# A 4-tokens-per-partition beginning and crossbar-DMA transposes in a fused gated-linear-attention and squared-ReLU kernel

## Chip, cores, metric

The kernel runs on one core of one Trainium2 chip. The metric is the device time of one execution in microseconds (us). A profile of one execution gives the span from the first to the last instruction, about 2 us shorter than the device time. Runs are classed as fast or slow (slow: more than 1.5% above the fastest of the same kernel); ratios, intervals and the times quoted below are of fast runs alone.

## The reference, cut to what matters

```python
# 4 batches x 8 heads x 768 tokens x 48: gated linear attention, token by token
for t in range(S):
    state = alpha[:, :, t, :, None] * state + einsum('bhd,bhe->bhde', k[:, :, t], v[:, :, t])
    y[:, :, t] = einsum('bhd,bhde->bhe', q[:, :, t], state)
x = y.transpose(0, 2, 1, 3).reshape(3072, 384)
h = x @ w_in                  # 384 x 2048
out = relu(h) ** 2 @ w_out    # 2048 x 384, float32 in and out
```

## The kernel before

The recurrence is cut into 24 chunks of 128 tokens (six for each batch). For each chunk, prefix sums of log alpha turn decay into products; q and k are scaled by them, transposed (eight 128x128 blocks), and multiplied to scores; masked scores times v, plus q times the carried state, give x; x is transposed (three blocks) and goes through the two matmuls of the feed-forward part, called the expert matmuls below. A planner in Python simulates the engines with fixed durations and emits every engine's instructions in the order that it found. That order is static: TensorE takes its matmuls in it, and waits where one is not ready.

```python
srcs = [(n, a.rearrange("b h (c p) d -> b c p h d", p=P)) for n, a in srcs]   # 128 tokens x 8 runs of 192 B
...
    d["ld_" + nm] = add("DMA", LD, ld, prev, lat=2.0, at=0.6)        # all DMAs on the SP queue, in order
...
        def e_p1():                                  # eight transposes by TensorE into PSUM
            d["pT"] = ps_misc.tile([P, 2 * NP, P], BF16, name="misc")
            for p in range(NP):
                tr(d["pT"][:, p, :], qA[:, 2 * p:2 * p + 2, :], ident_bf)
            for p in range(NP):
                tr(d["pT"][:, NP + p, :], kI[:, 2 * p:2 * p + 2, :], ident_bf)
        p1 = plan.add(Op("PE", 0.47, e_p1, [mq, mk], takes=[sl_misc], **g))
        def e_cp():                                  # and a VectorE copy to SBUF
            d["qkT"] = work.tile([P, 2 * NP, P], BF16, name="qkT")
            pin(nc.vector.tensor_copy(d["qkT"], d["pT"]))
...
        p2 = plan.add(Op("PE", 0.42, e_p2, [cp], takes=[sl_sc], **g))    # scores
...
    GN = [2, 1, 1, 2, 2, 2, 2, 2, 2, 2, 2, 2, 2]     # chunks in each group of expert matmuls
    DMA_ORDER = [0, 1, "i", "i", "i", "i", 2, 3, "o", "o", "o", "o"]   # chunks, w_in, w_out
# (all else cut)
```

Of the kernel before, what the change touches and what calls it, by code (L numbers as in the profile page):

```python
# [19 lines left out]
class Slots:  # L20
# [5 lines left out]
    def free_at(self):  # L26
        n = len(self.release) - self.bufs
        if n < 0:
            return 0.0
        op = self.release[n]  # L30
        return None if op.done is None else op.done
# [10 lines left out]
class Plan:  # L42
# [30 lines left out]
    def run(self, gate):  # L73
        free = self.free
        while any(self.pending.values()):
# [23 lines left out]
            if eng == "OUT":  # L99
                free["DMA"] = max(free.get("DMA", 0.0), t) + op.dur  # L100
# [6 lines left out]
        self.order.sort(key=lambda o: o.start)  # L107
# [3 lines left out]
def kernel(  # L111
# [21 lines left out]
    NT = n_tok // P  # L133

# [40 lines left out]

    NBUF = 4
    L_s = big.tile([P, NBUF, H, DP], BF16)
    nc.gpsimd.memset(L_s[:, :, :, D:], 0.0)
    qA_s = big.tile([P, NBUF, H, DP], BF16)
    nc.gpsimd.memset(qA_s[:, :, :, D:], 0.0)  # L180
    kI_s = big.tile([P, NBUF, H, DP], BF16)
    nc.gpsimd.memset(kI_s[:, :, :, D:], 0.0)
    ae_s = big.tile([P, NBUF, NP, 2], FP32)
    nc.vector.memset(ae_s, 0.0)  # L184
    xT_big = big.tile([P, KT, n_tok], BF16)
# [11 lines left out]
    sl_misc, sl_sc, sl_h, sl_o = Slots(2), Slots(1), Slots(2), Slots(1)  # L197
    X_SLACK = 0.3
    LD = 1.08
    WLD = 2.2  # L200
    SQ_PRIO = 0.0
# [8 lines left out]
    def cast(dst, box, j, d, n):  # L210
        def e_cast():
            eng = nc.vector if op.eng == "DVE" else nc.gpsimd
            pin(eng.tensor_copy(dst, box["t"][:, j, :]))  # L213
        op = add({"DVE": 0.06 + n / 1840.0, "POOL": 0.05 + n / 660.0}, 0, e_cast, d, prio=1.0)
        return op

    def load_w_in(i):
        w = d_ff // NWP
        sl = slice(i * w, (i + 1) * w)
        box = {}  # L220

        def ld():
            box["t"] = wload.tile([P, KT * d_ff // NWP], FP32, name="wst").rearrange("p (j n) -> p j n", j=KT)
            nc.sync.dma_start(out=box["t"], in_=w_in_r[:, :, sl])

        d = add("DMA", WLD, ld, lat=2.0)
        cs = []
        for j in range(KT):
            cs.append(cast(w_in_b[:, j, sl], box, j, d, 512))
        w_in_ready.append(cs)  # L230

    def load_w_out(i):
# [9 lines left out]
        for j in range(w):  # L242
            cs.append(cast(w_out_b[:, i * w + j, :], box, j, d, d_model))
# [6 lines left out]
    def add_loads(s):  # L250
        d = C[s]
        b, c = divmod(s, NCH)
        for nm, src in srcs:
# [3 lines left out]
            prev = C[s - LB]["use_" + nm] if s >= LB else None  # L257
            d["ld_" + nm] = add("DMA", LD, ld, prev, lat=2.0, at=0.6)

    def add_chunk(s):  # L260
        d = C[s]
        b, c = divmod(s, NCH)
# [5 lines left out]

        def e_ln():
            pin(nc.scalar.activation(L[:, :, 0:D], d["at"], AF.Ln))  # L270
        ln = d["use_at"] = add("ACT", 0.41, e_ln, d["ld_at"], old, prio=-5.0)
        ln.chunk = s

        def e_vb():
            d["vb"] = work.tile([P, H, D], BF16, name="vb", bufs=4)
            pin(nc.gpsimd.tensor_copy(d["vb"], d["vt"]))  # L276
        vb = d["use_vt"] = add("POOL", 0.62, e_vb, d["ld_vt"], old, prio=-1.0)

        def e_p0():
            pm = d["pm"] = ps_misc.tile([P, 512], FP32, name="misc")  # L280
            mm(pm[:, 0:HD], lhsT=utri_b[:, 0, :], rhs=L[:, :, 0:D], start=True, stop=True)
            for p in range(NP):
                mm(pm[:, HD + p:HD + p + 1], lhsT=L[:, 2 * p:2 * p + 2, :], rhs=ones_col,
                   start=True, stop=True)
        p0 = Op("PE", 0.28, e_p0, [ln], takes=[sl_misc], **g)
        p0.gla = s

        def exp(out_t, lo, hi, sl, scale):
            pin(nc.scalar.activation(out_t, sl, AF.Exp, scale=scale))

        def e_A():
            d["A"] = work.tile([P, H, D], BF16, name="A")
            pin(nc.scalar.activation(d["A"], d["pm"][:, 0:HD].rearrange("p (h d) -> p h d", h=H), AF.Exp))  # L293

        def e_Ai():
            d["Ai"] = work.tile([P, H, D], BF16, name="Ainv")
            pin(nc.scalar.activation(d["Ai"], d["pm"][:, 0:HD].rearrange("p (h d) -> p h d", h=H), AF.Exp, scale=-1.0))  # L297

        def e_ae0():
            pin(nc.scalar.activation(ae[0:64, :, 0], d["pm"][0:64, HD:HD + NP], AF.Exp))  # L300

        def e_ae1():
            pin(nc.scalar.activation(ae[64:128, :, 1], d["pm"][64:128, HD:HD + NP], AF.Exp))
        plan.add(p0)
        a_ = add("ACT", 0.39, e_A, p0, **g)
        ai = add("ACT", 0.38, e_Ai, p0, a_, **g)
        ae0 = add("ACT", 0.18, e_ae0, p0, ai, **g)
        ae1 = add("ACT", 0.19, e_ae1, p0, ae0, **g)
        p0.gives = ae1

        def e_qA():
            pin(nc.vector.tensor_mul(qA[:, :, 0:D], d["qt"], d["A"]))  # L312

        def e_kI():
            pin(nc.vector.tensor_mul(kI[:, :, 0:D], d["kt"], d["Ai"]))  # L315
        mq = d["use_qt"] = add("DVE", 0.47, e_qA, a_, d["ld_qt"], old, **g)
        mk = d["use_kt"] = add("DVE", 0.47, e_kI, ai, d["ld_kt"], old, **g)

        def e_p1():
            d["pT"] = ps_misc.tile([P, 2 * NP, P], BF16, name="misc")  # L320
            for p in range(NP):
                tr(d["pT"][:, p, :], qA[:, 2 * p:2 * p + 2, :], ident_bf)
            for p in range(NP):
                tr(d["pT"][:, NP + p, :], kI[:, 2 * p:2 * p + 2, :], ident_bf)
        p1 = plan.add(Op("PE", 0.47, e_p1, [mq, mk], takes=[sl_misc], **g))

        def e_cp():
            d["qkT"] = work.tile([P, 2 * NP, P], BF16, name="qkT")
            pin(nc.vector.tensor_copy(d["qkT"], d["pT"]))  # L329
        cp = add("DVE", 0.61, e_cp, p1, **g)  # L330
        p1.gives = cp

        def e_p2():
            sc = d["sc"] = ps_sc.tile([P, 2, NP, P], FP32, name="sc")
            t = d["qkT"]
            for p in range(NP):
                for hh in range(2):
                    sl = slice(64 * hh, 64 * hh + 64)
                    mm(sc[:, hh, p, :], lhsT=t[sl, NP + p, :], rhs=t[sl, p, :], start=True, stop=True)
        p2 = plan.add(Op("PE", 0.42, e_p2, [cp], takes=[sl_sc], **g))  # L340

        def e_sm(hh):
            if hh == 0:
                d["sm"] = work.tile([P, 2, NP, P], BF16, name="sm")
            pin(nc.vector.tensor_mul(d["sm"][:, hh], d["sc"][:, hh], utri_b.to_broadcast([P, NP, P])))  # L345
        sm0 = add("DVE", 0.6, lambda: e_sm(0), p2, **g)
        sm1 = add("DVE", 0.6, lambda: e_sm(1), p2, sm0, **g)
        p2.gives = sm1

        ps = None  # L350
        if not last:
            def e_ps():
                if c == 0:
                    state["ps"] = ps_st.tile([P, NP, 2 * D], FP32, name="st")
                st = d["st"] = state["ps"]
                for p in range(NP):
                    mm(st[:, p, :], lhsT=kI[:, 2 * p:2 * p + 2, :], rhs=d["vb"][:, 2 * p:2 * p + 2, :],
                       start=(c == 0 and p == 0), stop=True, skip_group_check=True)
            prev = C[s - 1].get("sb") if s else None
            if c == 0 and s:  # L360
                prev = C[s - 2]["sb"]
            ps = plan.add(Op("PE", 0.17, e_ps, [mk, vb, ae1, prev], **g))
# [11 lines left out]
        def e_p3():  # L374
            py = d["py"] = ps_misc.tile([P, 512], FP32, name="misc")
            if c > 0:
                for p in range(NP):
                    mm(py[:, 2 * p * D:2 * (p + 1) * D], lhsT=d["qkT"][:, p, :], rhs=C[s - 1]["sbt"][:, p, :],
                       start=(p == 0), stop=False, skip_group_check=True)
            for hh in range(2):  # L380
                for p in range(NP):
                    h = 2 * p + hh
                    mm(py[:, h * D:(h + 1) * D], lhsT=d["sm"][:, hh, p, :], rhs=d["vb"][:, h, :],
                       start=(c == 0 and hh == 0 and p == 0), stop=True, skip_group_check=True)
        p3 = plan.add(Op("PE", 0.39, e_p3, [sm1, vb, C[s - 1]["sb"] if c else None], takes=[sl_misc], **g))
# [7 lines left out]
        def e_p4():  # L393
            d["px"] = ps_misc.tile([P, KT, P], BF16, name="misc")
            for j in range(KT):
                tr(d["px"][:, j, :], d["xn"][:, j * P:(j + 1) * P], ident_bf)
        p4 = plan.add(Op("PE", 0.18, e_p4, [xn], takes=[sl_misc], **g))
# [8 lines left out]
    GN = [2, 1, 1, 2, 2, 2, 2, 2, 2, 2, 2, 2, 2]  # L406
# [4 lines left out]
    NQ = 4  # L411
    M1_ALT = 3
# [7 lines left out]
    def add_moe1(g, f, before):  # L420
# [17 lines left out]
        rl = add("ACT", (72 + n) / 1200.0, e_relu, op, prio=RELU_PRIO if g > 1 else RELU_PRIO0)  # L438
        op.gives = rl
        def e_sq():  # L440
            if f == 0:
                gT[g] = big.tile([P, FT, 384], BF16, name=f"gT{g % 3}", tag=f"gT{g % 3}")
            eng = nc.vector if sq[(g, f)].eng == "DVE" else nc.gpsimd
            pin(eng.tensor_mul(gT[g][:, f, 0:n], box["r"][:, 0:n], box["r"][:, 0:n]))  # L444
        fr = sq[(g - 3, "free")] if g >= 3 else None
        first = sq[(g, 0)] if f else None
        sq[(g, f)] = add({"DVE": 0.05 + n / 1900.0, "POOL": 0.06 + n / 440.0}, 0, e_sq, rl, fr, first, prio=SQ_PRIO)
        return op

    def add_moe2(g, tt, before):  # L450
# [3 lines left out]
        for qd in range(NQ):  # L454
            def e_mm(qd=qd, me=None):
# [3 lines left out]
                for kf in range(qd * FT // NQ, (qd + 1) * FT // NQ):  # L459
                    mm(box["po"], lhsT=gT[g][:, kf, tt * P:(tt + 1) * P], rhs=w_out_b[:, kf, :],  # L460
                       start=(kf == 0), stop=(kf == FT - 1))
            deps = [sq[(g, f)] for f in range(FT)] + sum(w_out_ready, []) + [before if qd == 0 else op]
            op = plan.add(Op("PE", 2.56 / NQ, e_mm, deps, takes=([sl_o, sl_misc] if tail else [sl_o]) if qd == 0 else None, prio=0.1, lat=0.2))
# [3 lines left out]

            op.lat = 0.0 if qd < NQ - 1 else 0.2

        def e_ev():  # L470
            box["ob"] = opool.tile([P, d_model], FP32, name="ob")
# [91 lines left out]
```

## Time and profile before

| | before |
|---|---|
| time, median of 4 runs | 200.94 us |
| span of the profiled run | 198.8 us |
| first w_in matmul | 17.62 us |
| first w_out matmul | 42.10 us |
| TensorE idle from 60 to 180 us | 0.8 us |
| DMA engines full | to about 130 us |

The table of stretches of the kernel before gives, for each stretch in us, the busy time of TensorE, its weight loads, VectorE, ScalarE and GpSimd (instructions in brackets), then the granted TensorE clock, the busy share of the DMA engines, and the rate.

```profile
20.00:40.00 20.00, 17.69 (x210) 13.07 (x209) 17.89 (x47) 14.30 (x53) 11.92 (x23) 0.97 0.99 248
...
80.00:100.00 20.00, 20.00 (x220) 14.98 (x218) 14.42 (x26) 15.51 (x47) 12.56 (x21) 1.00 1.07 197
...
120.00:140.00 20.00, 20.00 (x226) 15.17 (x225) 12.77 (x25) 14.62 (x45) 12.01 (x20) 1.00 0.67 124
...
160.00:180.00 20.00, 20.00 (x214) 15.22 (x212) 10.44 (x21) 12.96 (x39) 11.29 (x19) 1.00 0.09 32
```

From 80 us on TensorE is busy 20.00 of 20 us: whatever TensorE does there is the time. The DMA engines are full too until about 130 us, and hardly used after it. The next lines, from the timeline of the kernel before (start, length, engine, line, operation), mark its beginning: the first expert matmul, and the first one with w_out.

```profile
17.62 1.33 PE L191 MATMUL ph<-xT_big,w_in_b 128*128 128x256 bf16 x6 [1.34 <-DVE xT_big L400]
...
42.10 2.76 PE L191 MATMUL po<-w_out_b,gT_340 128*128 128x384 bf16 x16
```

The page of the kernel before shows what the DMA engines carry, and the chain of work that ended last:

```profile
DMA packets 107035, 30.23 MB, mean 152 GB/s; under 512 B 100353, under 2 KB 105473, under 8 KB 107009
...
q1 hardware_dynamic: 107008, 29.89, 72.7%
...
PE 78%; ACT 5%; DVE 5%; DMA 4%; SPq 4%; issue 2%; POOL 2%; ACTq 0%; POOLq 0%; DVEq 0%
```

Nearly all packets are the 192 B runs of q, k, v and alpha. The chain is TensorE for 78%.

### The profile page before, as it was taken

The numbers are of one execution on the slowest core, as the hardware profiler recorded it, in microseconds if no ns is written. First come the engines' busy times: TensorE is split into PE (matmuls) and PEld (weight loads), VectorE is DVE, ScalarE is ACT, GpSimd is POOL, SyncE is SP. The second block draws the span as 40 slices with busy tenths as digits, with TensorE's granted clock in tenths as the row PEclk, the third lists the DMA queues.
The fourth block names the chain that finished last, engine by engine and source line by source line (L and its number), as shares of the span: only waits on it lengthen the run. The fifth ranks groups of instructions, "written<-read, shape, count | busy, mean of one in ns | idle before, by whom it ended". The sixth has DMA issues, their size and how long they took to land.

```text
span 198.8 us, 5351 instructions
## 1 busy us (share of the span) xinstructions
PE 186.3 (94%) x1973; PEld 136.1 (68%) x1976; DVE 130.3 (66%) x265; ACT 131.8 (66%) x396; POOL 101.5 (51%) x175
## 2 busy tenths in 40 slices
PE   7876987989999899999999999999999999999993
PEld 3444745757577688777777777877777777777661
DVE  0775888977789897776666677665857756713300
ACT  3523864866569899767877877776886776656510
POOL 5134654841146757755666566576475464465300
PEclk9997899999999999999999999999999999999999
DMA  6999999898999999899999999851101101100022
GB/s 123 186 350 347 166 250 378 199 206 173 198 195 213 195 173 192 170 214 195 197 179 210 196 197 207 167 114 40 41 3 40 42 1 46 40 38 19 27 79 79
DMA packets 107035, 30.23 MB, mean 152 GB/s; under 512 B 100353, under 2 KB 105473, under 8 KB 107009
## 3 DMA queue, kind: packets, MB, share of 16 engines
q1 hardware_dynamic: 107008, 29.89, 72.7%
q8 instruction: 15, 0.25, 0.6%
q14 instruction: 12, 0.09, 0.2%
HBM read 25.17 MB, written 4.72 MB: 150 GB/s over the span
## 4 chain that ended last, share of the span: by engine, by line
PE 78%; ACT 5%; DVE 5%; DMA 4%; SPq 4%; issue 2%; POOL 2%; ACTq 0%; POOLq 0%; DVEq 0%
PE po L191 29%; PE ph L191 28%; PE misc L191 10%; PE misc L194 6%; DMA wst<-in_moe_w_in_dram 4%; PE sc L191 4%; SPq L256 3%; ACT r L437 3%; PE st L191 1%; DVE gT_606 L444 1%; DVE w_out_b L213 1%; DVE gT_752 L444 1%; POOL gT_340 L444 1%; DVE qkT L329 1%; POOL gT_1148 L444 1%
## 5 line engine op out<-in xcount | busy, mean ns | idle before, releaser
L437 ACT ACTIVATE r<-ph 128x256 bf16<-128x256 f32 (+1 forms) x192 | 67.5, 374 | 30.7 <-PE ph L191 25.9
L191 PE MATMUL ph<-xT_big,w_in_b 128*128 128x256 bf16 (+1 forms) x576 | 81.6, 269 | 2.4 <-DVE xT_big L400 1.3
L191 PEld LDWEIGHTS <-w_in_b 128*128 128x128 bf16 x624 | 54.1, 99 | 17.3 <-issue 3.6
L345 DVE TENSOR_TENSOR sm<-sc,utri_b 128x512 bf16<-128x512 f32 x48 | 31.6, 685 | 5.2 <-PE sc L191 5.0
L276 POOL CAST vb<-vt 128x384 bf16<-128x384 f32 x24 | 13.3, 553 | 17.5 <-DMA vt<-in_v_dram 17.5
L312 DVE TENSOR_TENSOR qA_s<-qt,A 128x384 bf16<-128x384 f32 x24 | 13.9, 579 | 11.8 <-ACT A L293 11.4
L329 DVE COPY qkT<-misc 128x1024 bf16<-128x1024 bf16 x24 | 16.5, 689 | 5.6 <-PE misc L194 4.8
L293 ACT ACTIVATE A<-misc 128x384 bf16<-128x384 f32 x24 | 11.7, 488 | 9.0 <-PE misc L191 9.0
L315 DVE TENSOR_TENSOR kI_s<-kt,Ainv 128x384 bf16<-128x384 f32 x24 | 16.5, 687 | 1.1
L191 PEld LDWEIGHTS <-qkT 64*128 64x128 bf16 (+1 forms) x272 | 10.6, 95 | 7.0 <-DVE qkT L329 1.6
L270 ACT ACTIVATE L_s<-at 128x384 bf16<-128x384 f32 x24 | 12.5, 522 | 3.8 <-DMA at<-in_alpha_dram 3.7
L475 ACT COPY ob<-po 128x384 f32<-128x384 f32 x20 | 9.6, 478 | 6.6 <-PE po L191 6.2
L400 DVE COPY xT_big<-misc 128x384 bf16<-128x384 bf16 x24 | 8.5, 354 | 8.1 <-PE misc L194 8.0
L389 ACT CAST xn<-misc 128x384 bf16<-128x384 f32 x24 | 11.5, 479 | 3.2 <-PE misc L191 3.1
L191 PE MATMUL po<-warm 128*128 128x512 bf16 x37 | 10.9, 424 | 1.6 <-DVE ae_s L184 1.3
L371 ACT CAST sb<-st 128x384 bf16<-128x384 f32 x20 | 9.5, 477 | 3.9 <-DVE st L366 3.7
L297 ACT ACTIVATE Ainv<-misc 128x384 bf16<-128x384 f32 x24 | 12.0, 499 | 0.0
L366 DVE TENSOR_TENSOR st<-st,ae_s 128x384 f32<-128x384 f32 x20 | 11.1, 556 | 0.4 <-PE st L191 0.4
L444 POOL TENSOR_TENSOR gT_3206<-r 128x256 bf16<-128x256 bf16 x12 | 7.6, 639 | 6.2 <-ACT r L437 5.3
L444 POOL TENSOR_TENSOR gT_2317<-r 128x256 bf16<-128x256 bf16 x12 | 7.6, 639 | 5.7 <-ACT r L437 4.8
L444 POOL TENSOR_TENSOR gT_2008<-r 128x256 bf16<-128x256 bf16 x12 | 7.6, 639 | 5.6 <-ACT r L437 4.9
L444 POOL TENSOR_TENSOR gT_2923<-r 128x256 bf16<-128x256 bf16 x12 | 7.6, 642 | 5.5 <-ACT r L437 5.0
(92 smaller groups left out, 349.5 us busy)
## 6 DMA issues: line engine op xcount, KB each, us to landing
at<-in_alpha_dram SPq DMA_DIRECT2D x24, 192.0 KB, 4.3
qt<-in_q_dram SPq DMA_DIRECT2D x24, 192.0 KB, 4.3
kt<-in_k_dram SPq DMA_DIRECT2D x24, 192.0 KB, 4.6
vt<-in_v_dram SPq DMA_DIRECT2D x24, 192.0 KB, 4.2
out_dram<-ob SPq DMA_DIRECT2D x24, 192.0 KB, 2.1
wst<-in_moe_w_in_dram SPq DMA_DIRECT2D x4, 768.0 KB, 8.5
wst<-in_moe_w_out_dram SPq DMA_DIRECT2D x4, 768.0 KB, 8.9
```

What stands on the lines that cost most here:

```text
L191: pin(nc.tensor.matmul(*a, **kw))
L194: pin(nc.tensor.transpose(*a))
L270: pin(nc.scalar.activation(L[:, :, 0:D], d["at"], AF.Ln))
L276: pin(nc.gpsimd.tensor_copy(d["vb"], d["vt"]))
L293: pin(nc.scalar.activation(d["A"], d["pm"][:, 0:HD].rearrange("p (h d) -> p h d", h=H), AF.Exp))
L297: pin(nc.scalar.activation(d["Ai"], d["pm"][:, 0:HD].rearrange("p (h d) -> p h d", h=H), AF.Exp, scale=-1.0))
L312: pin(nc.vector.tensor_mul(qA[:, :, 0:D], d["qt"], d["A"]))
L315: pin(nc.vector.tensor_mul(kI[:, :, 0:D], d["kt"], d["Ai"]))
L329: pin(nc.vector.tensor_copy(d["qkT"], d["pT"]))
L345: pin(nc.vector.tensor_mul(d["sm"][:, hh], d["sc"][:, hh], utri_b.to_broadcast([P, NP, P])))
L437: pin(nc.scalar.activation(box["r"][:, 0:n], box["ph"][:, 0:n], AF.Relu))
L444: pin(eng.tensor_mul(gT[g][:, f, 0:n], box["r"][:, 0:n], box["r"][:, 0:n]))
```

## The change

Two ideas, both to take work or waiting from TensorE. First, the first chunks of all four batches need no state, so they are done together at the start, in a layout of four tokens to a partition: q, k and alpha then come in runs of 768 B, and four chunks of x are ready for the expert matmuls. Second, from the ninth chunk on, q, k and x are transposed by crossbar DMAs from SBUF to SBUF. The diff, cut to its core:

```diff
+    order = [b * NCH for b in range(B)] + [b * NCH + c for b in range(B) for c in range(1, NCH)]
+    QK_DMA = 8
+    X_DMA = 8
+    TR_LAT = 2.5                     # the planner's latency of a transpose after its 0.9 or 0.34 us
+    AHEAD = 3.0
-        self.order.sort(key=lambda o: o.start)
+        self.order.sort(key=lambda o: o.start - (ahead if o.eng == "DMA" else 0.0))
+    def add_first_loads(nm, ap, tag):
+            F[nm] = big.tile([P, H, J * D], FP32, name="first_" + nm, tag=tag)
+            src = ap[:, :, 0:P, :].rearrange("b h (i j) d -> b i h (j d)", j=J)
+            w = P // B
+            for b in range(B):
+                nc.sync.dma_start(out=F[nm][b * w:(b + 1) * w], in_=src[b])   # a band of 32 partitions
 ... (prefix sums over four tokens a partition, four chunks at once; k transposed back; masks: cut)
+            def e_tr():
+                d["qkT"] = work.tile([P, 2 * NP, P], BF16, name="qkT")
+                nc.sync.dma_start_transpose(out=d["qkT"], in_=qk_s[:, i].rearrange("p x h d -> p (x h d)"))
+            if s >= QK_DMA:
+                cp = add("TR", 0.9, e_tr, mq, mk, lat=TR_LAT, prio=-20.0)
+                return ae1, mk, [cp]
+        def e_trx():
+            nc.sync.dma_start_transpose(out=xT_big[:, :, s * P:(s + 1) * P], in_=d["xn"])
+        if s >= X_DMA:
+            d["x"] = d["end"] = add("TR", 0.34, e_trx, xn, lat=TR_LAT + X_SLACK, prio=-20.0)
+            return
-    GN = [2, 1, 1, 2, 2, 2, 2, 2, 2, 2, 2, 2, 2]
+    GN = [1, 1, 2, 2, 2, 2, 2, 2, 2, 2, 2, 2, 2]
-    DMA_ORDER = [0, 1, "i", "i", "i", "i", 2, 3, "o", "o", "o", "o"]
+    DMA_ORDER = ["v", "i", "i", "i", "i", 4, "o", "o", "o", "o"]
 ... (w_out matmuls of the first groups in two halves; casts on more engines: cut)
```

## The prediction

> **What bounds it now.** Two regimes. The table of stretches shows TensorE busy 20.0 of 20 us in every stretch from 80 to 180 us, and the chain of waits runs 78% on TensorE. So from about 45 us to the end the time is the sum of TensorE work. Before that TensorE waits: the timeline has its first expert matmul at 17.6 us (two chunks and four w_in pieces had to land first; dummies fill the gaps) and its first w_out matmul at 42.2 us. From matmul spacing in the timeline (one token tile: 16 w_out matmuls of 0.163 us and its share of w_in, 5.2 us; recurrence 1.8 us a chunk) useful work is about 24 x 7.0 = 168 us (estimate). The 198.8 us span therefore loses about 27 us, 3.4 of it at the tail and nearly all the rest before 42 us. DMA is full until about 130 us, at only 195 GB/s, because 100353 of 107035 packets are under 512 B; one 192 KB load then costs about 1.0 us, a chunk 4 us.
>
> **The change.**
> 1. *Beginning.* The first chunk of all four batches comes first; they need no state. q, k and alpha come in 768 B runs; at the 350 to 377 GB/s that the weight stretches show that is 2.2 us per tensor of four chunks, not 4. v stays at 1 us a load. Before the last w_in piece: 6.6 + 4 + 8.8 = 19.4 us of DMA, against 16.8 now. So the first expert matmul does not come earlier (18 to 20 us). But then four tiles, not two, are ready, and with half of w_out their second matmuls start (about 30 us, not 42). Added: block cumulative sums and k transposed back, about 3 us of TensorE. Estimated idle before saturation: 12 to 15 us instead of 24. Gain 9 to 12, less 3 of added work: 6 to 9 us.
> 2. *Transposes.* The timeline has eight q/k transposes taking 0.45 us of TensorE and three x transposes 0.17: 0.62 us a chunk, times 16 = 9.9 us, all in the saturated stretch. VectorE also loses 0.69 + 0.35 us of copies a chunk, which isn't critical.
> 3. *Cost.* 352 KB a chunk go through the DMA engines. The Trainium skill (DMA: Bandwidth & Descriptors, Latency and other measured facts) gives transposes 261 GB/s: an estimated 1.35 us a chunk, 22 us in all. DMA per chunk becomes 4.0 + 0.55 + 1.35 = 5.9 us, under TensorE's 6.4. No run here shows it yet. Latency is the danger: loads take 4.3 us from issue to landing on the same in-order queue, a transpose behind them probably 4 to 5, where the schedule allows 3.4. TensorE's order is fixed, so score matmuls may wait 0 to 1 us a chunk: I allow 4 us in all.
>
> **Prediction.** 168 + 3 - 10 = 161 us of work, 13 idle at the start, 3.4 tail, 4 of new waits: span about 181, time (2 us above the span) **183 us**, range **175 to 196**. Faster by over 2%: **0.90**; within 2%: **0.05**; slower: **0.05**.
>
> **Right if:** first w_out matmul near 30 us; TensorE full from about 36 us; matmul count down by about 176 for the transposes and up by some 70 at the start; each transpose DMA landing within about 5 us; DMA busy until 150 us or later; waits of TensorE for qkT or xT_big under 0.5 us each.
>
> **Wrong if:** transposes block other traffic or run far below 261 GB/s (two or three times the cost makes DMA, not TensorE, the limit and the gain vanishes); the SP queue, waiting for q/k products, holds loads back; or the 32-partition first loads run well below weight-load rate, which delays the start.

## The result, and the profile after

The time rose to 208.75 us (median of 4 runs, 208.0 to 209.67), against 200.94 us: ratio 1.039, 95% interval 1.034 to 1.044. Ratios are the mean time of one kernel's fast runs over that of the other's of the same rounds, so they are not quite the ratio of the medians quoted. The results are correct.

| | before | after |
|---|---|---|
| first w_in matmul | 17.62 us | 25.70 us |
| first w_out matmul | 42.10 us | 46.71 us |
| TensorE idle, 60 to 180 us | 0.8 us | 11.5 us |
| TensorE busy from 60 us to the end | 134.6 us | 133.1 us |
| DMA engines full | to 130 us | to about 160 us |

The same stretches of the changed kernel, and the page's lines on its DMA traffic and chain that answer to those shown before:

```profile
20.00:40.00 20.00, 17.83 (x225) 11.88 (x225) 16.72 (x41) 14.24 (x49) 10.47 (x19) 1.00 1.03 326
...
80.00:100.00 20.00, 17.65 (x168) 12.95 (x167) 12.32 (x30) 13.42 (x42) 5.72 (x9) 0.91 1.09 180
...
120.00:140.00 20.00, 17.82 (x190) 13.16 (x187) 13.03 (x31) 15.03 (x44) 4.99 (x8) 1.00 0.99 190
...
160.00:180.00 20.00, 17.98 (x179) 13.21 (x180) 12.73 (x28) 12.92 (x40) 3.91 (x6) 0.91 0.52 96
```

```profile
DMA packets 121369, 35.98 MB, mean 173 GB/s; under 512 B 111616, under 2 KB 119808, under 8 KB 121344
...
q1 hardware_dynamic: 121344, 35.66, 86.1%
...
PE 69%; DMA 20%; DVE 4%; ACT 3%; issue 1%; SPq 1%; ACTq 0%; DVEq 0%
```

TensorE, full before, now misses 2 us and more in each of these late stretches, and DMA has gone from 4% to 20% of the chain. The chain by line names the transposes: qkT 8.6% and xT_big 5.9% of the span. The timeline of the changed kernel shows its beginning,

```profile
25.70 0.34 PE L230 MATMUL po<-xT_big,w_in_b 128*128 128x128 bf16 x3
...
46.71 1.46 PE L230 MATMUL misc<-w_out_b,gT_398 128*128 128x384 bf16 x8
```

8 us and 4.6 us later than before, and one stall near the end of its loads (in time order, VectorE, SP and TensorE):

```profile
155.48 0.94 DVE L495 TENSOR_TENSOR qk_s<-kt,Ainv 128x384 bf16<-128x384 f32 x1
...
156.19 0.42 SPq L313 DMA_DIRECT2D qt<-in_q_dram  x1
...
156.72 2.06 SPq L507 DMA_TRANSPOSE qkT<-qk_s  x1
...
159.57 0.24 PE L230 MATMUL misc<-ones_col,L_s 128*128 128x1 bf16 x4
...
162.01 0.26 PE L230 MATMUL sc_3114<-qkT 64*128 64x128 bf16 x1 [2.21 <-DMA qkT<-qk_s]
...
162.53 1.46 PE L230 MATMUL po<-w_out_b,gT_2877 128*128 128x384 bf16 x4
```

The k product ends at 156.42 (155.48 + 0.94), SP issues the transpose at 156.72 but needs 2.06 us to get it into the queues, and the scores start 5.6 us after the product. The schedule had allowed 3.4 us (0.9 + 2.5). Over the sixteen chunks this distance is 3.2 to 5.9 us, median 4.6. The bracket says that TensorE sat idle 2.21 us. The last line shows a second price: four w_out matmuls take 1.46 us, where 0.81 is the normal length. The narrow stretches around it show the granted clock (column before the last two):

```profile
159.00:160.00 1.00, 0.81 (x9) 0.46 (x7) 0.58 (x2) 0.79 (x4) 0.00 (x0) 1.00 1.32 236
...
161.00:162.00 1.00, 0.00 (x0) 0.00 (x0) 0.00 (x0) 0.27 (x1) 0.00 (x0) 1.00 1.24 211
...
163.00:164.00 1.00, 1.00 (x6) 0.45 (x3) 1.00 (x3) 0.00 (x0) 0.00 (x0) 0.50 1.20 261
```

After the 2.21 us of idle the clock is at half for 3.4 us. It happened twice after 60 us (the other after a wait of 2.35 us that ended at 86 us); the clock of 0.91 in two of the 20 us stretches is that, 1.7 us of TensorE time each. The Trainium skill (TensorE: Matmul & The Clock Gate, Why this matters for your kernels) tells to leave no idle gaps over about 3 us; here 2.2 us was enough. The length of one gap doesn't decide it: among the runs below, half clock followed waits of 1.44 and 0.60 us close together in stride_tr (at 146.5 us), and did not follow a wait of 2.04 us in tr_lat5 (ended at 102.6 us).

From 60 us on the sums are: 9.9 us of transposes gone from TensorE, but about 4.9 us of work left over from the slower beginning (measured below without the transposes) and 3.4 us of half clock; so its busy time fell only 1.5 us, and its idle time rose by 10.7 us. That is the 9.2 us between the spans.

### The profile page after: what moved, and what is told of

Its sections match the earlier page's. It is cut to its first block, busy times and chain, and to the rows that moved or that the text cites. A ratio compares the mean times of both kernels' runs of the same rounds, so it can differ in the third digit from the quotient of the medians.

```text
span 208.0 us, 5075 instructions
## 1 busy us (share of the span) xinstructions
PE 184.7 (89%) x1816; PEld 131.0 (63%) x1817; DVE 130.8 (63%) x309; ACT 136.6 (66%) x399; POOL 61.1 (29%) x112
## 4 chain that ended last, share of the span: by engine, by line
PE 69%; DMA 20%; DVE 4%; ACT 3%; issue 1%; SPq 1%; ACTq 0%; DVEq 0%
PE ph L230 26%; PE po L230 23%; PE misc L230 11%; DMA qkT<-qk_s 9%; DMA xT_big<-xn 6%; DMA first_k_154<-in_k_dram 4%; PE misc L233 2%; DMA first_a_144<-in_alpha_dram 2%; ACT r L668 1%; PE st L230 1%; DVE qk_s L395 1%; DVE gT_398 L675 1%; DVE gT_642 L675 1%; SPq L326 1%; PE sc_289 L230 0%
## 5 line engine op out<-in xcount | busy, mean ns | idle before, releaser
L449 POOL CAST vb<-vt 128x384 bf16<-128x384 f32 x20 | 11.6, 578 | 13.8 <-DMA vt<-in_v_dram 10.8
L495 DVE TENSOR_TENSOR qk_s<-kt,Ainv 128x384 bf16<-128x384 f32 x20 | 14.3, 715 | 0.3
L613 ACT CAST xn<-misc 128x384 bf16<-128x384 f32 x24 | 11.5, 479 | 3.4 <-PE misc L230 3.4
L590 DVE TENSOR_TENSOR st<-st,ae_s 128x384 f32<-128x384 f32 x20 | 11.2, 561 | 1.4 <-PE st L230 1.2
L723 ACT COPY ob<-po 128x384 f32<-128x384 f32 x16 | 7.7, 481 | 6.0 <-PE po L230 5.8
L473 ACT ACTIVATE A<-misc 128x384 bf16<-128x384 f32 x20 | 9.8, 492 | 2.3 <-PE misc L230 2.1
L492 DVE TENSOR_TENSOR qk_s<-qt,A 128x384 bf16<-128x384 f32 x20 | 11.0, 552 | 0.6 <-ACT A L473 0.5
L455 ACT ACTIVATE L_s<-at 128x384 bf16<-128x384 f32 x20 | 10.5, 523 | 0.1
L477 ACT ACTIVATE Ainv<-misc 128x384 bf16<-128x384 f32 x20 | 9.9, 493 | 0.0
L675 DVE TENSOR_TENSOR gT_3625<-r 128x256 bf16<-128x256 bf16 x16 | 4.6, 292 | 7.5 <-ACT r L668 7.3
L675 POOL TENSOR_TENSOR gT_1744<-r 128x256 bf16<-128x256 bf16 x5 | 3.6, 730 | 13.6 <-ACT r L668 11.6
L675 POOL TENSOR_TENSOR gT_1163<-r 128x256 bf16<-128x256 bf16 x7 | 4.9, 716 | 8.5 <-ACT r L668 8.5
L230 PE MATMUL po<-w_out_b,gT_2877 128*128 128x384 bf16 x32 | 7.4, 358 | 0.0
L230 PE MATMUL po<-w_out_b,gT_1464 128*128 128x384 bf16 x32 | 7.2, 353 | 0.0
L233 PEld LDWEIGHTS <-qk_s 128*128 128x128 bf16 x64 | 5.1, 116 | 3.2 <-DVE qk_s L395 2.3
```

The source lines that it names most:

```text
L230: pin(nc.tensor.matmul(*a, **kw))
L449: pin((nc.vector if vb.eng == "DVE" else nc.gpsimd).tensor_copy(d["vb"], src))
L455: pin(nc.scalar.activation(L[:, :, 0:D], d["at"], AF.Ln))
L473: pin(nc.scalar.activation(d["A"], d["pm"][:, 0:HD].rearrange("p (h d) -> p h d", h=H), AF.Exp))
L477: pin(nc.scalar.activation(d["Ai"], d["pm"][:, 0:HD].rearrange("p (h d) -> p h d", h=H), AF.Exp, scale=-1.0))
L492: pin(nc.vector.tensor_mul(qA[:, :, 0:D], d["qt"], d["A"]))
```

## The experiments

Fifteen kernels ran. "Idle" is the idle time of TensorE from 60 to 180 us, from the table of stretches. The last kernel, the probe, does other work and is not in the table. The letters of theories and rivals belong to the run that they stand with: rival B of qk_only is not rival B of lat4.

| kernel | time, us | ratio to before | 95% interval | idle, us |
|---|---|---|---|---|
| before | 200.8 to 201.6 | 1 | | 0.8 |
| the change | 208.75 | 1.039 | 1.034 to 1.044 | 11.5 |
| start_only | 204.87 | 1.019 | 1.013 to 1.025 | 0.6 |
| tr_only | 208.29 | 1.035 | 1.029 to 1.042 | 13.2 |
| qk_only | 209.46 | 1.041 | 1.034 to 1.048 | 10.5 |
| x_only | 207.20 | 1.031 | 1.025 to 1.038 | 4.6 |
| lat4 (two fast runs) | 207.38 | 1.033 | 1.026 to 1.039 | 11.0 |
| lat5 | 212.94 | 1.059 | 1.056 to 1.062 | 12.8 |
| tr_lat5 | 207.96 | 1.037 | 1.033 to 1.041 | 13.8 |
| stride_start | 202.19 | 1.008 | 1.004 to 1.012 | 0.6 |
| cheap_base (wrong) | 198.30 | 0.987 | 0.984 to 0.990 | 0.6 |
| cheap_tr (wrong) | 194.75 | 0.970 | 0.967 to 0.973 | 7.2 |
| tr_late | 198.79 | 0.990 | 0.987 to 0.994 | 1.7 |
| dummy_tr | 204.75 | 1.017 | 1.011 to 1.023 | 4.5 |
| stride_late | 201.08 | 0.999 | 0.993 to 1.004 | 1.2 |
| stride_tr | 207.77 | 1.030 | 1.022 to 1.037 | 12.0 |

### One half of the change at a time: start_only and tr_only

start_only is the changed kernel with `QK_DMA = X_DMA = 99`. tr_only is the kernel before with the transposes added (the lines of the diff with `e_tr`, `e_trx` and the new sorting, which come with them; tr_late below has the same sorting and is faster than before, so the sorting is not the loss).

> The changed kernel with every transpose back on TensorE; only the new beginning is left. Theory L (transposes land later than the fixed order of TensorE allows, 11 us of idle after 60 us, and the beginning is about 5 us behind at 60 us): no idle after 60 us (under 1.5 us), 10 us more of transposes on TensorE, time 203 to 207. Rival S (the slow beginning is the whole loss, the transposes are worth what they should be, 10 us): time 214 to 219.

> The kernel before with its old beginning and only the transposes of chunks 8 to 23 moved to DMA. Theory L: TensorE idles 10 us or more after 60 us on qkT and xT_big and its clock falls after the longest waits, so time 201 to 206. Rival S: transposes are a gain by themselves, time 190 to 194.

start_only was as theory L expected. Its TensorE is full from 80 us on (first row below), but from 60 us to its end it is busy 139.5 us, 4.9 us more than before: that much is left over from the beginning. tr_only was over both theories' ranges: the transposes alone, on the old beginning, cost 7.5 us where I had promised a gain of 10. So rival S is out. Of the tables of stretches, one row of start_only and two of tr_only:

```profile
80.00:100.00 20.00, 19.97 (x223) 15.26 (x221) 16.56 (x37) 15.31 (x48) 8.28 (x14) 1.00 1.12 208
...
80.00:100.00 20.00, 16.55 (x157) 11.36 (x155) 8.09 (x17) 11.74 (x35) 8.04 (x13) 0.91 1.03 177
...
140.00:160.00 20.00, 16.32 (x168) 12.17 (x165) 10.14 (x20) 14.57 (x42) 9.13 (x15) 0.99 0.98 184
```

Over 3 us are missing in each row of tr_only, with DMA full. The waits of tr_only put 13.4 us of TensorE's idle on qkT.

### q and k, or x: qk_only and x_only

```diff
-    QK_DMA = 8        # x_only: 99
-    X_DMA = 8         # qk_only: 99
```

> The changed kernel with only q and k by DMA, x transposed by TensorE again (16 x 0.17 = 2.7 us more TensorE work). Theory L: the q/k transposes, the larger and with the least slack, make most of the idle: time 206 to 210. Rival B (what costs is the DMA and SP queue time of the transposes, in proportion to bytes): x is 27% of the bytes, so a quarter of the loss against the new beginning alone goes away.

> The changed kernel with only x by DMA, q and k transposed by TensorE again. x has slack before its matmul, so theory L expects little idle and a small gain over the new beginning alone: 1 to 3 us less than start_only. If the x transposes also stall TensorE (chain of waits of the changed kernel has 5.9% on them), it is equal to or above start_only.

Each of the two costs: against start_only of the same rounds qk_only is 4.6 us slower and x_only 2.3 us slower, though each takes work from TensorE. For x_only my expected gain was a miss: xT_big makes TensorE wait up to 1.7 us. The loss is not tied to the slack of one step. It does not follow the bytes either: both together cost 3.9 us over start_only (208.75 of other rounds against 204.87), no more than qk_only alone within the noise (ratios 1.039 and 1.041), so taking x away did not remove a quarter of the loss.

### More latency in the schedule: lat4, lat5, tr_lat5

```diff
-    TR_LAT = 2.5
+    TR_LAT = 4.0      # lat4; lat5: 5.5; tr_lat5 (on tr_only): 5.0
```

> The changed kernel; the schedule's figure for a transpose's latency is 4.0 us instead of 2.5, which puts the score matmuls 1.5 us later in the order of TensorE. In the changed kernel the scores start 4.2 to 5.9 us after the k product ends while loads run, and the schedule allows 3.4. Theory L (TensorE stalls because its order is too early): most of the 11 us of idle after 60 us goes, time 198 to 203. Rival B (the DMA engines and the SP queue cannot carry loads and transposes at the pace of TensorE, so waiting only moves): time 206 to 211, the idle stays.

> As the run before, with 5.5 us. Theory L: idle after 60 us under 3 us, time 196 to 201 (new beginning alone 204.9, less 10 us of TensorE transposes, plus a little). Rival B: 206 to 212.

> The old beginning, transposes of chunks 8 to 23 by DMA, the schedule's latency 5.0 us. Theory L: the old kernel less 10 us of TensorE work with little idle, time 191 to 196, faster than both kernels. Rival B: 205 to 210 as with 2.5 us.

Theory L fell in its simple form: none gained clear of noise (lat4's ratio of 1.033 and the change's of 1.039 have overlapping intervals), lat5 lost 4 us more, just over the range that rival B gave, and the idle stayed at 11 to 14 us. The timeline shows where the added time went. In the changed kernel the SP queue issues a q/k transpose 0.07 us (median) after the k product is done. In lat5 it issues it 2.7 us after (median, at most 5.1), since the queue is still busy with what stands ahead. Here is the SP queue of lat5 from one q/k transpose to the next:

```profile
112.65 1.51 SPq L507 DMA_TRANSPOSE qkT<-qk_s  x1
114.20 0.58 SPq L313 DMA_DIRECT2D kt<-in_k_dram  x1
114.89 0.60 SPq L313 DMA_DIRECT2D vt<-in_v_dram  x1
115.58 1.62 SPq L622 DMA_TRANSPOSE xT_big<-xn  x1
117.26 0.57 SPq L313 DMA_DIRECT2D at<-in_alpha_dram  x1
117.88 0.57 SPq L313 DMA_DIRECT2D qt<-in_q_dram  x1
118.55 0.88 SPq L728 DMA_DIRECT2D out_dram<-ob  x1
119.54 1.29 SPq L507 DMA_TRANSPOSE qkT<-qk_s  x1
```

A chunk's seven DMAs fill the queue without a gap for 6.9 us, and this is one of the shortest of its rounds: from 78.66 to 152.76 us the q/k transposes of lat5 are issued 8.2 us apart on average. TensorE's own work on a chunk, without the transposes, is 6.4 us (an estimate: in the kernel before, with TensorE full, the scores of successive chunks come 7.05 us apart from 80.8 to 172.4 us, less 0.62 of transposes). A path that is slower than its user eats any head start: that is rival B.

### What each form of DMA costs by itself: probe

A kernel of DMAs alone: sixteen loads of each form, transposes, a mixture of a chunk's four loads and two transposes, and the beginning's loads in two layouts. Theory Q, named in the expectation, is that loads and transposes together ask for more DMA time than TensorE takes for a chunk; it is tested under cheap_base. The 261 GB/s are the figure cited in the prediction.

> DMA forms alone, one section after another; output zeros, wrong on purpose. Per transfer, in a row of its kind: a 192 KB load in 192 B runs about 1.0 us; contiguous 0.55 to 0.6; a q/k transpose (256 KB) 1.0 if transposes run at 261 GB/s, 1.4 to 2.0 if theory Q's sum (7 us of DMA a chunk) is right; an x transpose (96 KB) 0.38 or 0.5 to 0.8; a chunk's four loads with both transposes 5.4 or over 6. The beginning's 768 KB tensor: 3.5 to 4 us into bands of 32 partitions, 2.2 to 2.7 into every fourth partition.

The framework let DMAs of a later section go early, so the sections overlap at their edges and only their middle is used. Loads in 192 B runs: fifteen landings in 14.0 us, 0.94 us each. Contiguous: 0.5 us each, about the pace at which SP issues them (0.47). Transposes in a row could not be timed cleanly: alone, SP needs about 1.25 us to issue either kind, which is the pace. The mixture, on the SP queue of the probe, and the stretch that it spans:

```profile
41.42 1.75 SPq L63 DMA_TRANSPOSE mixq<-src  x1
...
47.28 1.56 SPq L63 DMA_TRANSPOSE mixq<-src  x1
...
53.44 1.48 SPq L63 DMA_TRANSPOSE mixq<-src  x1
...
41.42:53.44 12.02, 0.62 (x4) 0.00 (x0) 1.00 1.02 199
```

The three q/k transposes stand 12.0 us apart for two rounds: 6.0 us for a chunk's four loads and its two transposes, at a DMA share of 1.02. Four loads alone are 3.8 us, so two transposes add 2.2 us: 360 KB at 160 GB/s. The Trainium skill (DMA: Bandwidth & Descriptors, Latency and other measured facts) gives 261 GB/s for a non-contiguous middle dimension, and another page (Advanced Engine Details and Errata, X-Bar Transpose (TRN2)) that transposes are as fast as regular DMAs; next to small loads neither was reached. With the chunk's output (0.5 us in the probe's closing row of 24 stores) the sum is 6.5 us, over TensorE's 6.4, before any waiting in order. In the changed kernel eleven q/k transposes, issued from 80.65 to 156.72 us, stand 7.6 us apart. So most of its deficit is not in the probe's sum. Over these 76.1 us the DMA share is 1.02; SP spends 67.6 us issuing, 6.8 a chunk, of which 2.05 for each q/k transpose against some 1.6 in the mixture, and the remaining 8.5 us are gaps, 3.8 of them before q/k transposes, where SP stands until the product is ready and the loads behind stand too. The prediction had named that danger; it is the smaller part.

The same probe gives the beginning. These are the VectorE copies that saw each 768 KB tensor land, first into bands of 32 partitions, then into every fourth partition:

```profile
70.50 0.15 DVE L46 COPY tok<-band 128x1 f32<-128x1 f32 x1 [1.58 <-DMA band<-in_q_dram]
74.08 0.15 DVE L46 COPY tok<-band 128x1 f32<-128x1 f32 x1 [3.43 <-DMA band<-in_k_dram]
...
82.29 0.15 DVE L94 COPY tok<-stride 128x1 f32<-128x1 f32 x1 [2.65 <-DMA stride<-in_k_dram]
84.91 0.15 DVE L94 COPY tok<-stride 128x1 f32<-128x1 f32 x1 [2.46 <-DMA stride<-in_k_dram]
```

3.6 us for a tensor in bands, 2.6 us spread over all partitions, 2.8 for the one ahead of it, a quarter of which had landed early (the releaser names both k, as the sections' loads follow one another). SP needs some 0.6 us to issue each spread quarter, so 2.6 us is also its own pace.

### The beginning mended: stride_start

```diff
-                nc.sync.dma_start(out=F[nm][b * w:(b + 1) * w], in_=src[b])
+                nc.sync.dma_start(out=F[nm][b:P:B], in_=src[b])
# and the masks and the transposes' column order to match; QK_DMA = X_DMA = 99
```

> The new beginning alone (all transposes on TensorE), but the four batches take every fourth partition instead of a band of 32, so each load of the beginning writes to partitions across the whole range. In the changed kernel the four tensors of the beginning (3.1 MB) come at 180 to 200 GB/s where weights come at 350 and more. Theory P (a load into 32 adjacent partitions is slow because it reaches only part of the write paths): alpha, q, k land sooner, 2 to 5 us off, time 200 to 203. Rival R (768 B runs themselves are slow): same rate, 204 to 206.

Theory P held: 202.19 against 204.87 us in the other rounds, ratios 1.008 and 1.019 to the same kernel. The first expert matmul comes at 23.41 us (24.91 and 24.10 in stride_late and stride_tr, which begin alike; 26.39 in start_only). The Trainium skill (SBUF — State Buffer, Door 1: The DMA port swizzle) says that DMA bandwidth depends on how many of 16 ports the partitions reach; by its table 32 adjacent partitions reach 8. From 5 to 10 us, while these tensors load, the changed kernel moves 202 GB/s and stride_start 279; in the changed kernel q and k land 3.9 us after the tensor before each, in stride_start 3.0. But the mended beginning is still 0.8% slower than the old one: from 60 us on TensorE is busy 136.3 us, 1.7 more than before. The added prefix sums and back-transposes, which I had put at 3 us, seem not to be paid back; no run takes them out alone.

### Room on the DMA engines: cheap_base, cheap_tr, tr_late

```diff
-    srcs = [(n, a.rearrange("b h (c p) d -> b c p h d", p=P)) for n, a in srcs]
+    srcs = [(n, a.rearrange("b h s d -> (b h s d)").rearrange("(n p x) -> n p x", p=P, x=HD)) for n, a in srcs]
# cheap_base on the kernel before, cheap_tr on tr_only: same bytes, contiguous, wrong results on purpose
-    QK_DMA = 8
-    X_DMA = 8
+    QK_DMA = 18
+    X_DMA = 17
# tr_late, on tr_only, with the right loads
```

> The kernel before, wrong on purpose: each chunk's loads take the same number of bytes from contiguous memory (1536 B a partition instead of eight runs of 192 B), so they take less of the DMA engines. The base for the next run. Expected 194 to 200, TensorE as full after 60 us as before.

> The same contiguous loads, with the transposes of chunks 8 to 23 by DMA at the schedule's latency of 2.5 us (wrong on purpose). Theory Q (loads and transposes together ask for more of the DMA engines than a chunk's TensorE time, so transposes queue behind loads and loads behind transposes): with room on the engines, scores start 3.3 to 3.8 us after the k product, idle after 60 us falls under 4 us, time 6 to 10 us below cheap_base. Rival F (it is the fixed latency and the in-order SP queue, whatever the loads): no gain, time within 2 us of cheap_base or above.

> The kernel before (correct), with DMA transposes only after its loads have ended near 128 us: q and k from chunk 18 on, x from chunk 17 on. Theory Q: latency 3.3 us as the schedule allows, little idle, 6 x 0.45 + 7 x 0.17 = 3.9 us less TensorE work, time 196.5 to 198.5, faster than both kernels. Rival F: idle eats it, 200 to 203.

With cheap loads the sign turns: the same transposes that cost 7.5 us now gain 3.5 us (194.75 against 198.30). Nothing in the transposes or in the schedule was altered. That is under the 6 to 10 us expected, with 7.2 us of idle where under 4 was expected. The rows, of cheap_base first and then of cheap_tr, show where: 4.7 us of it lies between 60 and 100 us, where the DMA share with transposes is still 0.77 and 0.94 (3.9 us there are waits for qkT), 0.9 from 100 to 120 us, and 1.5 near the end. From 120 to 160 us TensorE is full.

```profile
80.00:100.00 20.00, 20.00 (x224) 15.20 (x223) 14.33 (x27) 14.93 (x45) 12.03 (x20) 1.00 0.56 165
...
80.00:100.00 20.00, 17.62 (x179) 12.74 (x177) 11.58 (x22) 13.96 (x42) 9.36 (x16) 1.00 0.94 212
...
120.00:140.00 20.00, 19.96 (x204) 14.90 (x203) 13.16 (x25) 15.87 (x47) 10.44 (x16) 1.00 0.58 143
```

tr_late does correct work and beats both kernels: 198.79 us, 0.990 of before, clear of noise (0.987 to 0.994) though inside the 2% that count as the same. Its transposes start at 134.27 us, when the loads have ended (the last lands at 131.4). They land 3.1 to 3.3 us after issue (3.0 to 5.3 in the changed kernel), each takes SP 1.23 us instead of a median of 1.8, and TensorE stays full:

```profile
120.00:140.00 20.00, 19.10 (x203) 13.93 (x202) 10.61 (x21) 13.59 (x42) 11.11 (x19) 1.00 0.54 118
...
160.00:180.00 20.00, 20.00 (x195) 14.84 (x193) 10.26 (x19) 13.28 (x39) 10.15 (x16) 1.00 0.31 76
```

It is 0.3 us above its expected range: of 3.9 us of transposes 2.1 became time, 0.9 us was lost in the stretch from 120 to 140 us, in a wait of 0.5 us for the first xT_big and one of 0.4 us for an output copy of ScalarE.

### The traffic without the wait: dummy_tr

```diff
-            cp = add("TR", 0.9, e_tr, mq, mk, lat=TR_LAT, prio=-20.0)
+            add("TR", 0.9, e_tr, mq, mk, lat=TR_LAT, prio=-20.0)     # into an unread tile; x likewise
+        p1 = plan.add(Op("PE", 0.47, e_p1, [mq, mk], takes=[sl_misc], **g))   # TensorE transposes all
```

> The kernel before with TensorE doing every transpose, and the DMA transposes of chunks 8 to 23 issued as well, at the same places of the SP queue, into tiles that nobody reads. It carries the DMA traffic of the transposes but no step waits for a transpose. Theory W (the loss is that TensorE waits for transposes that sit in full queues): within 1.5% of before, 200 to 204, idle of TensorE after 60 us under 2 us. Rival T (the traffic by itself makes the loads late and starves the kernel): 205 or more, with waits on loads.

It fell between the theories: 204.75 us, 3.2 us over the kernel before of the same rounds. The traffic by itself costs. A row of its table of stretches and its waits on ScalarE name it:

```profile
100.00:120.00 20.00, 16.35 (x179) 11.93 (x177) 12.01 (x23) 12.17 (x38) 9.34 (x16) 1.00 1.11 193
...
ACT L_s L272 <- DMA at<-in_alpha_dram: 8.0, 3, 4.1
```

Three times ScalarE waits for alpha, up to 4.1 us, and TensorE loses 3.65 us between 100 and 120 us; then it is full again. So the transposes make loads late, as rival T says. The rest of tr_only's idle, 13.2 us against 4.5 here, goes with TensorE's own waits for transposes that sit in full queues, as theory W says. The split is not exact: dummy_tr keeps 0.62 us more TensorE work a chunk, which leaves the DMA path more time.

### The two mendings together: stride_late and stride_tr

stride_late is stride_start with `QK_DMA = 18, X_DMA = 17`; stride_tr is stride_start with both at 8, so the change with only its layout mended.

> The new beginning with every fourth partition for a batch, and DMA transposes only after the loads have ended (q and k from chunk 18, x from 17). If the two mendings add up: 202.2 less the 2 us that the late transposes gave the old beginning, 199.5 to 201, equal to the kernel before or up to 1% faster, and not better than the old beginning with late transposes (198.8).

> The whole change with only the partition layout of the beginning mended. If the start and the transposes are separate losses, it keeps the whole 2.7 us of the mending: 205 to 207. If the loss is the pace of the DMA engines from 60 us on, an earlier start only meets the same queue sooner and little of it is kept: 207 to 209.

stride_late, 201.08 us, is equal to the kernel before, and not better than tr_late. stride_tr, 207.77 us, keeps about 1 us of the 2.7: its ratio of 1.030 (interval 1.022 to 1.037) and the change's of 1.039 (1.034 to 1.044) have overlapping intervals, so how much of the mending is kept is not settled. It fits what the first two runs left odd, that losses of 4.1 and 7.5 us make only 7.8 together: when the DMA path sets the pace, a later start is partly hidden behind it.

## Why the prediction was wrong

- **What bounds the kernel before.** Right: two regimes, TensorE full from about 45 us; a microsecond of TensorE work added or left over there came out as time (start_only: 4.9 us more work, 4.1 us more time).
- **"2.2 us per tensor of four chunks", and "First expert matmul 18 to 20 us".** Wrong. The rate was taken from the weights, which reach all partitions. In bands of 32 partitions the tensors took about 3.6 us in the probe and 3.9 in the changed kernel, and the first expert matmul came at 25.7 us. The last w_in piece landed at 29.1 us against 20.9 before, 8.2 us later where my sums of DMA gave 2.6 (19.4 against 16.8); three tensors at 3.9 instead of 2.2 are 5.1 us of that. I had named this as a risk and given it no weight in the sum. Mending it gave 2.7 us.
- **"Gain 9 to 12, less 3 of added work: 6 to 9 us" for the beginning.** Wrong even with the layout mended: start_only lost 4.1 us, stride_start 1.3. The first w_out matmul came at 46.7 us (44.4 mended), not near 30. I counted the w_out loads as early enough: SP issued the first at 29.68 us, half of w_out had landed at 38.2 us and its casts ended near 44, so 30 was out of reach whatever x did. Nor did I follow the chain from the last first load, through four chunks' products, transposes, scores and masks, to x: in the changed kernel k lands at 14.5 us and the first expert matmul starts 11.2 us later (10.9 in stride_start). How much each of the two costs in time was not measured apart.
- **"0.62 us a chunk, times 16 = 9.9 us".** The work did leave TensorE; that part is right, and tr_late turned a share of it into time.
- **"DMA per chunk becomes 4.0 + 0.55 + 1.35 = 5.9 us, under TensorE's 6.4".** This is the step that failed. The term mis-sized is the 1.35 us: next to small loads two transposes took 2.2 us, so the sum is 6.5 us and no longer under TensorE's 6.4. And the sum left the in-order queue out: in the kernel a chunk took 7.6 us, with SP issuing for 6.8 of it. A margin of 0.5 us on a resource that was already full became a deficit. The page's 261 GB/s was taken over for a mixture that it does not speak of.
- **"TensorE's order is fixed, so score matmuls may wait 0 to 1 us a chunk: I allow 4 us in all".** The mechanism was right, the size off: 10.7 us of idle, plus 3.4 us at half clock after the longest stalls, which I had not counted at all. And it was no matter of latency that a later place in the order could mend: lat4, lat5 and tr_lat5 show that.
- **"Each transpose DMA landing within about 5 us".** Nearly right (3.0 to 5.3), and useless as a test: the schedule had allowed 3.4 from product to scores, so landings of this size already meant stalls.
- **Chances.** 0.05 for slower was too low. Among what would make it wrong I had written "transposes ... run far below 261 GB/s (two or three times the cost makes DMA, not TensorE, the limit and the gain vanishes)". 1.6 times was enough, since nothing was left to absorb it.

What stays open: in the mixture the DMA engines (share 1.02) and the SP queue are full at once. No run here separates the engines' time from the issuing time, which is 1.2 us a transpose even with nothing beside it; cheap_tr and tr_late relieve both. A kernel whose transposes are issued by another engine than SP would tell, and was not run.

## What to carry to other kernels

Before moving work from a full engine to DMA, add up the DMA path for one period of the steady state, with durations from the same mixture of packets, issuing time and outputs included, and compare it with the period of the engine that is relieved; a few per cent of margin on a path that is already full is none. If more latency in a schedule is eaten by the queue and the idle stays, the limit is throughput. The same DMAs can pay where the engines have room: here only after the loads had ended.

## What the Trainium skill lacked or had wrong

- DMA: Bandwidth & Descriptors (Latency and other measured facts) and Advanced Engine Details and Errata (X-Bar Transpose (TRN2)): no figure for SBUF-to-SBUF transposes beside loads in small runs. Here 360 KB of transposes added 2.2 us to four loads in 192 B runs (160 GB/s, SP's issuing included), not 261 GB/s or the pace of regular DMAs.
- DMA: Bandwidth & Descriptors (Issuing engines are not separate DMA queues) calls the sequencer's time to initiate a DMA "usually small relative to the DMA itself". A transpose held the SP queue 1.23 us alone and up to 3.3 us behind loads, against 0.43 for a load that met no queue.
- TensorE: Matmul & The Clock Gate (Why this matters for your kernels): gaps over about 3 us are named as harmful. Here idle gaps of 2.21 and 2.35 us were each followed by 3.4 us at a granted clock of 0.50, and a gap of 2.04 us in tr_lat5 was not.
- SBUF — State Buffer (Door 1: The DMA port swizzle) is right and was the page to read: 3.6 us for 768 KB in bands of 32 partitions, 2.6 us spread. It does not name a spread by a partition step as the remedy.
- VectorE: DVE Perf Modes (The three transpose paths) compares one 128x128 block (390 ns on TensorE, 1309 ns by DMA). In a stream TensorE needed 0.45 us for eight blocks, and a DMA of eight blocks landed in 3.1 to 3.3 us with the queues empty; that page has neither.
